# Closing waits of SyncE moved ahead of its fifth last output transfer

## The chip, the cores and the metric

The kernel runs on one core of a Trainium2 chip. The core has five engines with an instruction queue each: TensorE (PE), VectorE (DVE), ScalarE (ACT), GpSimd (POOL) and SyncE (SP). SyncE computes nothing: it issues transfers (DMAs) and waits. Engines and transfers are ordered by semaphores: an instruction raises one when it is done, a transfer raises its own by 16 when it has landed, and an engine that needs the result holds its queue until the semaphore has the value. The metric is the device time of one execution in microseconds. Before the change it was 160.47 us, the median of three runs (159.72, 160.47 and 160.56).

## The reference

The input x has 2048 rows of 448 values in bfloat16. It is normalized (`xn`), and two branches work on xn. Branch A is a linear recurrence with 448 complex states; branch B normalizes again and is a two-layer perceptron with 1792 hidden values. The result joins them with x:

```python
def _A_ref(x, Lambda_re, Lambda_im, B_re, B_im, C_re, C_im, log_dt, Dskip):
    Lam = Lambda_re + 1j * Lambda_im
    Lam_bar = jnp.exp(jnp.exp(log_dt) * Lam)
    Bu = jnp.einsum("bld,pd->blp", x + 0j, ((Lam_bar - 1.0) / Lam)[:, None] * (B_re + 1j * B_im))
    for t in range(L):
        h = Lam_bar[None, :] * h + Bu[:, t, :]        # collected in hseq
    return 2.0 * jnp.einsum("blp,dp->bld", hseq, C_re + 1j * C_im).real + x * Dskip
def _B_ref(x, w1, b1, w2, b2):
    h = gelu(jnp.einsum("bsd,df->bsf", layernorm(x), w1) + b1)
    return jnp.einsum("bsf,fd->bsd", h, w2) + b2
xn = layernorm(x)
out = x + _A_ref(xn, ...) * silu(_B_ref(xn, ...))
```

## The kernel before, in words

The 2048 rows are worked in four groups of 512, each in two blocks of 256 rows, and each block in its even and its odd rows. For a group the kernel normalizes the rows, transposes them by DMA (line 83), runs the perceptron's two layers on TensorE (lines 735 and 754), projects into the states (line 663), scans over time on VectorE, and multiplies the states back (`ym`, lines 787 to 793). `ym` ends with a product with the gate (line 796), a sum (line 799) and an output transfer (lines 808 and 813). A block's even and odd rows leave in one transfer of 224 KB, except in the last block, which leaves in three: 112 KB and 64 KB by SyncE's queue, 48 KB by ScalarE's.

No scheduler decides the order when the program is built. Every piece of work is recorded as a `Task` with the engine that does it and the buffers that it reads and writes; `link` turns these into dependences. `emit` walks a fixed list of task numbers, `ORDER`, and writes each task's instructions into its engine's queue. Ahead of a task it writes a wait for each semaphore that the task needs and that its engine hasn't yet waited for (lines 120 to 123); `seen` remembers, for each engine, how far it has waited. Each transfer has a semaphore of its own, named d0, d1 and so on (lines 76 to 85), so SyncE never learns of most transfers: the engines that read the data wait for them.

After the last task, lines 135 to 137 have SyncE wait for every semaphore at its final value that it hasn't already waited for. This is the closing list: 58 waits, which the build packs two to an instruction, so 29 instructions. Behind it stands the end of the block (line 288): a drain on SyncE and a barrier of all engines, released by GpSimd.

SyncE's queue ends with seven output transfers. The first two of these carry group 1. The other five are the two blocks of group 2 and the first block of group 3 (224 KB each), and the 112 KB and 64 KB of the last block. Each waits for the addition that makes its data. The last output transfer of the kernel, 48 KB, stands in ScalarE's queue.

Of the kernel before, what the change touches and what calls it, by code (L numbers as in the profile page):

```python
# [14 lines left out]
ENGS = ("pe", "act", "dve", "pool", "sp")  # L15
# [20 lines left out]
class Plan:  # L36
# [69 lines left out]
    def emit(self):  # L106
        self.link()
        for k in SECOND:
            self.tasks[k].choose(1)
        order = [self.tasks[k] for k in ORDER]  # L110
        assert len(order) == len(set(order)) == len(self.tasks)
        done = {}
        for t in order:
            eng, seen = self.engs[t.eng], self.seen[t.eng]
            need = {}
            for d in t.deps:
                sem, val = done[d]
                if need.get(sem, 0) < val:
                    need[sem] = val
            for sem, val in need.items():  # L120
                if seen.get(sem, 0) < val:
                    eng.wait_ge(self.sems[sem], val)
                    seen[sem] = val
            for k, fn in enumerate(t.ins):
                last = fn(eng)
                if t.chain and k < len(t.ins) - 1:
                    self.counts[t.eng] += 1
                    last.then_inc(self.sems[t.eng], 1)
                    eng.wait_ge(self.sems[t.eng], self.counts[t.eng])
                    seen[t.eng] = self.counts[t.eng]  # L130
            inc = 16 if t.sem not in ENGS else 1
            self.counts[t.sem] += inc
            last.then_inc(self.sems[t.sem], inc)
            done[t] = (t.sem, self.counts[t.sem])
        for sem, val in self.counts.items():
            if val and self.seen["sp"].get(sem, 0) < val:
                self.nc.sync.wait_ge(self.sems[sem], val)
# [781 lines left out]
```

## Time and profile before

| what | value |
|---|---|
| time, median of three runs | 160.47 us (159.72 to 160.56) |
| span of the profiled execution, first to last instruction | 158.54 us |
| last record of the same execution, from its first instruction | 160.47 us |
| TensorE busy | 148.2 us (93%) |
| VectorE busy | 136.2 us (86%) |
| end of the last VectorE addition | 155.81 us |
| issue of SyncE's last five output transfers | 140.62, 148.22, 153.76, 155.10, 155.62 us |
| issue of ScalarE's output transfer, and its landing | 155.85, 157.43 us |
| closing waits (line 137) | 29 instructions, 156.01 to 158.28 us |
| SyncE's drain at the block's end | 158.31 us |

Times are counted from the first instruction. "Issue" is when the queue starts the transfer's instruction; the landing is the last of its semaphore's 16 raises. A wait instruction is recorded from the moment its semaphores are met and the queue takes it, and takes 0.028 us itself. The page doesn't count waits and issues as busy time. The time of a whole execution is longer than its span, since work of the runtime lies around it: the semaphores are reset behind the last instruction, and the last such record is the one in the table.

### The profile page before, as it was taken

The page shows a single profiled execution, that of the slowest core. Times are in us where ns is not written, and L with a number is a line of the kernel's source. Part 1 is how long each engine was busy: PE and PEld are TensorE (multiplying, and loading weights), DVE is VectorE, ACT ScalarE, POOL GpSimd, SP SyncE. Part 2 cuts the span into 40 slices and gives each one's busy share as a digit, 9 for nine tenths or more (in the row PEclk, how much of TensorE's full clock was granted, in tenths as well). Part 3 has the DMA queues.
Part 4 walks back from the last instruction along what each step waited for, and adds up shares of the span by engine and source line. Part 5 has one row for each costly group of instructions (what it writes and reads, how often), then busy time and mean ns, then how long its engine had stood idle before and what let it go on. Part 6 is the DMA issues. An engine that isn't in the chain of part 4 may idle for free.

```text
span 158.5 us, 3106 instructions
## 1 busy us (share of the span) xinstructions
PE 148.2 (93%) x1130; PEld 87.9 (55%) x1130; DVE 136.2 (86%) x295; ACT 96.7 (61%) x180; POOL 38.8 (24%) x94
## 2 busy tenths in 40 slices
PE   0989999699999999999999999999999999999990
PEld 0977765244456656665554555675545665555560
DVE  1789997489898999989899799748999969999692
ACT  3589888998699667688989070233395774224110
POOL 5528622031902000054000018530000450002311
PEclk9999999999999999999999999999999999999998
DMA  4999966999998530000000517202740000010103
GB/s 110 269 300 290 316 187 130 202 233 246 110 170 166 60 76 0 2 0 0 4 0 0 102 27 160 80 0 45 51 142 0 0 4 0 0 58 4 58 2 118
DMA packets 31238, 14.75 MB, mean 93 GB/s; under 512 B 24752, under 2 KB 30774, under 8 KB 31222
## 3 DMA queue, kind: packets, MB, share of 16 engines
q1 hardware_dynamic: 30912, 14.26, 41.0%
q0 software_dynamic: 160, 0.23, 0.7%
q8 instruction: 9, 0.15, 0.4%
q10 hardware_dynamic: 150, 0.05, 0.1%
q14 instruction: 7, 0.06, 0.1%
HBM read 6.89 MB, written 1.84 MB: 55 GB/s over the span
## 4 chain that ended last, share of the span: by engine, by line
PE 67%; DMA 13%; SPq 9%; DVE 5%; issue 2%; ACT 2%; DVEq 0%
PE psum L754 20%; PE psum L735 15%; PE psum L663 14%; PE psum L787 10%; SPq L84 7%; DMA Bn<-in_A_B_im_dram 7%; PE psum L652 3%; PE psum L790 3%; DMA x_all<-in_A_x_dram 3%; DMA xnT<-xn_sb 3%; SPq L83 2%; ACT gT L739 1%; DVE t L796 1%; DVE tmp L799 1%; DVE o L757 1%
## 5 line engine op out<-in xcount | busy, mean ns | idle before, releaser
L735 PE MATMUL psum<-xn2T,w_sb 64*128 64x512 bf16 (+1 forms) x462 | 45.4, 345 | 2.3 <-DMA xn2T<-xn_sb 1.5
L754 PE MATMUL psum<-w_sb,gT 128*128 128x448 bf16 x224 | 44.5, 353 | 0.2 <-issue 0.2
L739 ACT ACTIVATE gT<-psum,b1f 128x512 bf16<-128x512 f32 (+1 forms) x66 | 36.1, 621 | 5.7 <-PE psum L735 5.3
L735 PEld LDWEIGHTS psum<-xn2T,w_sb 64*128 64x128 bf16 x462 | 25.1, 109 | 20.6 <-issue 2.5
L754 PEld LDWEIGHTS psum<-w_sb,gT 128*128 128x128 bf16 x224 | 21.6, 98 | 20.6 <-issue 0.8
L663 PE MATMUL psum<-xnT,BT 128*128 128x256 bf16 x196 | 24.1, 273 | 0.3 <-ACT gT L739 0.3
L663 PEld LDWEIGHTS psum<-xnT,BT 128*128 128x128 bf16 x196 | 18.6, 98 | 6.4 <-issue 1.6
L384 ACT ACTIVATE u_sb<-psum 128x512 bf16<-128x512 f32 (+2 forms) x21 | 9.9, 470 | 14.0 <-PE psum L663 13.9
L758 ACT ACTIVATE th<-o 128x448 f32<-128x448 f32 x16 | 9.1, 576 | 9.7 <-DVE o L757 9.6
L384 ACT ACTIVATE vs<-s_w 64x256 bf16<-64x256 f32 (+2 forms) x14 | 7.9, 565 | 11.4 <-DVE s_w L689 7.5
L771 POOL TENSOR_TENSOR xr<-xd,g_sb 128x448 f32<-128x448 bf16 x4 | 4.8, 1194 | 41.2 <-DVE tmp L799 23.2
L687 DVE TENSOR_TENSOR_SCAN s_w<-dk,vs 128x774 f32<-128x774 f32 x8 | 13.9, 1760 | 0.0
L796 DVE TENSOR_TENSOR t<-psum,g_sb 128x448 bf16<-128x448 f32 (+2 forms) x17 | 10.0, 590 | 4.3 <-PE psum L790 2.2
L459 ACT ACTIVATE xn_sb<-x_all,lnw 128x448 bf16<-128x448 bf16 (+2 forms) x18 | 11.4, 672 | 3.5 <-POOL xd L771 2.1
L787 PE MATMUL psum<-CZ,h_sb 128*128 128x448 bf16 x56 | 11.9, 353 | 0.0
L698 POOL TENSOR_TENSOR ang<-s_w,ang 128x16 f32<-128x16 f32 x3 | 2.0, 675 | 40.3 <-ACT s_w L696 20.7
L757 DVE TENSOR_TENSOR o<-psum,b2bc 128x448 f32<-128x448 f32 x16 | 9.8, 616 | 1.5 <-PE psum L754 1.5
L759 DVE SCALAR_TENSOR_TENSOR g_sb<-th,o 128x448 bf16<-128x448 f32 x16 | 10.4, 649 | 0.3 <-ACT th L758 0.2
L787 PE MATMUL psum<-CQ,h_sb 128*128 128x448 bf16 (+2 forms) x54 | 10.5, 332 | 0.0
L372 DVE BATCH_NORM_STATS2 lnst<-x_all 128x6 f32<-128x448 bf16 x12 | 7.4, 622 | 1.2 <-DMA x_all<-in_A_x_dram 1.2
L613 ACT ACTIVATE tmp<-Cr,cw 128x448 f32<-128x448 bf16 (+1 forms) x10 | 6.5, 664 | 2.6 <-DVE CZ L616 1.3
L787 PEld LDWEIGHTS psum<-CZ,h_sb 128*128 128x128 bf16 x56 | 5.4, 98 | 4.9 <-DVE o L757 0.4
(161 smaller groups left out, 194.1 us busy)
## 6 DMA issues: line engine op xcount, KB each, us to landing
out_dram<-tmp SPq DMA_DIRECT2D x7, 224.0 KB, 2.0
x_all<-in_A_x_dram SPq DMA_DIRECT2D x3, 448.0 KB, 5.1
w_sb<-in_B_w_dram SPq DMA_DIRECT2D x3, 448.0 KB, 8.7
w_sb<-in_B_w_dram SPq DMA_DIRECT2D x3, 384.0 KB, 5.4
vs<-in_A_C_re_dram SPq DMA_DIRECT2D x1, 392.0 KB, 7.6
vs<-in_A_C_im_dram SPq DMA_DIRECT2D x1, 336.0 KB, 10.8
Bn<-in_A_B_re_dram SPq DMA_DIRECT2D x1, 336.0 KB, 11.0
Bn<-in_A_B_im_dram SPq DMA_DIRECT2D x1, 336.0 KB, 11.3
```

The costliest lines, as they stand in the source:

```text
L84: return e.dma_start(out_ap, in_ap)
L384: kb.either(("act", [lambda e, o=o, i=i: e.activation(o, i, ACT.Copy) for o, i in pairs]), ("dve", [lambda e, o=o, i=i: e.tensor_copy(o, i ...
L459: ("act", [lambda e, o=o, i=i: e.activation(o, i, ACT.Identity, bias=nb, scale=rs) for o, i in parts], 0.75, 0.2)]
L663: fns = [lambda e, r=r, m=m, d=d: e.matmul(psum[:, 4, r * NK:(r + 1) * NK], BT[:, m, d, :], xnT[:, gx, d, :], start=(d == 0), stop=(d == 6 ...
L687: dve(lambda e, so=so, vi=vi: e.tensor_tensor_scan(so, dk[:].rearrange("p i c -> p (i c)"), vi, 0.0, ALU.mult, ALU.add), ["v", "vl", "dk", ...
L735: return lambda e: e.matmul(view(bk[k]), w1_sb[rows, d, fcol(2 * j + k)], rhs[rows, d, :, :], start=not second and n == 0, stop=second and ...
L739: act([lambda e, k=k: e.activation(gT[:, gb, 2 * j + k, :].rearrange("p (r c) -> p r c", r=2)[:, :, cols], view(bk[k]), ACT.Gelu_apprx_tan ...
L754: fns = [lambda e, fi=fi: e.matmul(psum[:, bk, 0:D], gT[:, gb, fi, q * 128:(q + 1) * 128], w2_sb[:, fi, :], start=(fi == 0), stop=(fi == N ...
L757: dve(lambda e: e.tensor_tensor(o2[:, fb, :], psum[:, bk, 0:D], b2bc[:], ALU.add), [f"ps{bk}", "b2bc"], [f"oo{fb}"], 0.62, prio - 76)
L759: dve(lambda e: e.scalar_tensor_tensor(out=g_sb[:, gs, :], in0=th[:, fb, :], scalar=1.0, in1=o2[:, fb, :], op0=ALU.add, op1=ALU.mult), [f" ...
L787: fns = [lambda e, k=k: e.matmul(psum[:, bk, c0:c1], h_sb[:, hb, k, k0:k0 + 128], cm[:, k, c0:c1], start=(k == 0), stop=False) for k in ra ...
L796: dve(lambda e: e.tensor_tensor(t3[:, fb, c0:c1], psum[:, bk, c0:c1], g_sb[:, gs, c0:c1], ALU.mult), [f"ps{bk}", f"g{gs}"], [f"t3{fb}_{c0} ...
```

## The change

`emit` picks the fifth last task of SyncE in the order (`settle`). When the walk comes to it, SyncE first waits for every transfer semaphore raised so far by the walk that it has not waited for, at its value then; semaphores of the engines (`ENGS`) are left out. `seen` records these waits, so the closing list at the end leaves them out. The order of the tasks on every engine is the same.

```diff
@@ -110,8 +110,14 @@
         order = [self.tasks[k] for k in ORDER]
         assert len(order) == len(set(order)) == len(self.tasks)
         done = {}
+        settle = [t for t in order if t.eng == "sp"][-5]
         for t in order:
             eng, seen = self.engs[t.eng], self.seen[t.eng]
+            if t is settle:
+                for sem, val in self.counts.items():
+                    if val and sem not in ENGS and seen.get(sem, 0) < val:
+                        eng.wait_ge(self.sems[sem], val)
+                        seen[sem] = val
             need = {}
             for d in t.deps:
                 sem, val = done[d]
```

## Prediction

> **What bounds the kernel now.** I read the page's first lines for the balance, then the chain of work that ended last, then SyncE's waits from 115 us on, and last the source lines of the closing waits (L137), of the block's end (L288) and of the output transfers.
>
> ```profile
> span 158.5 us, 3106 instructions
> PE 148.2 (93%) x1130; PEld 87.9 (55%) x1130; DVE 136.2 (86%) x295; ACT 96.7 (61%) x180; POOL 38.8 (24%) x94
> PE 67%; DMA 13%; SPq 9%; DVE 5%; issue 2%; ACT 2%; DVEq 0%
> ```
>
> TensorE is busy for 93% of the span and has most of the chain: it bounds the body, and the change touches none of its work. What matters is the tail. The end of the chain:
>
> ```profile
> 154.69 0.38 DVE tmp L799
> 155.07 0.28 DVE t L796
> 155.35 0.03 issue
> 155.38 0.02 DVEq L122
> 155.40 0.04 issue
> 155.44 0.37 DVE tmp L799
> ```
>
> The last engine work ends at 155.81, and 2.7 us remain in which no engine computes. They hold the last transfers, the closing waits and the block's end. By source line (start of first and last behind the durations):
>
> ```profile
> L137 SPq EVENT_SEMAPHORE  x29: 27/28/28, 156.0 to 158.2; - x29
> ...
> L288 SPq DRAIN  x1: 13/13/13, 158.3 to 158.3; - x1
> L288 SPq EVENT_SEMAPHORE  x1: 17/17/17, 158.5 to 158.5; - x1
> ```
>
> The output transfers from 155.7 us on, with the time to landing:
>
> ```profile
> L84 ACTq DMA_DIRECT2D out_dram<-tmp x1: 379/379/379, 155.8 to 155.8; - x1
> ...
> DMA to landing us min/median/max: 1.6/1.6/1.6
> ```
>
> ScalarE's transfer is issued at 155.85 and has landed at 157.43 by the trace's landing records; SyncE's last one (issued at 155.62) landed at 157.22. But the 29 closing waits run from 156.01, the last starts at 158.25, and the drain behind it at 158.31. So the last output has been in memory for 0.82 us when SyncE reaches its wait: 14 wait instructions start after 157.43, all on semaphores met long before. The tail is bound by SyncE walking its list.
>
> SyncE's waits from 115 us on:
>
> ```profile
> SPq L84 <- DVE tmp L799: 37.1, 3, 24.7
> SPq L84 <- DVE pa L681: 2.5, 1, 2.5
> SPq L84 <- DVE t L796: 1.3, 1, 1.3
> SPq L84 <- POOL tmp L799: 0.2, 1, 0.2
> ```
>
> The longest, 24.7 us, ends with the transfer at 140.62, the fifth last of SyncE: the place to which the waits go.
>
> **The change part by part.** The profile gives a span of 158.54 us; the last record of that execution stands 160.47 us after its first instruction, like the median of the three runs (159.72, 160.47, 160.56). I set the sum against 160.47, with 1.93 us around the span unchanged.
>
> *Taken from the end.* 58 waits stand two to an instruction. SyncE's order in the two programs shows what stays behind its last transfer: five instructions (nine waits: the last six output transfers and the final counts of TensorE, VectorE and ScalarE). 24 of 29 go. In the profile the steady ones start 0.062 us apart; the first seven stand 0.064 to 0.095 apart, and between the seventh (156.45) and the eighth (156.95) lies a pause of 0.43 us above that pace. Counted as instructions alone, 24 x 0.062 = 1.49 us, with the pause 1.9 us. But the landing now ends last, so not all of that is won.
>
> *What is late next.* The five remaining waits begin at 156.01 as before. By the landing records their transfers land at 155.72 and before, 156.76, 157.22 and 157.43, so four of the five are over before the last landing. The last then follows 0.02 us behind it: no row shows SyncE held here, but its wait at 22.79 us began 0.017 us after the landing at 22.776, and VectorE's and ScalarE's follow such landings by 0.02 to 0.03. Bounds: 0.017 us, and 0.095 if a full wait step comes on top; I take 0.02, from the rows of the same event. From there as now: 0.028 for the wait, 0.037 to the drain, 0.225 from the drain's start to the span's end. The new end is 157.425 + 0.02 + 0.028 + 0.037 + 0.225 = 157.735: 0.80 us less than 158.539 (0.73 at the upper bound).
>
> *Added ahead of the fifth last transfer.* 49 waits, 48 of them in 25 instructions (one more instruction on SyncE in all) and one riding on the transfer; the last of the 25 also holds the transfer's wait for VectorE. SyncE ends the issue before at 115.95 and is idle until 140.62. The youngest transfers waited for are the two outputs issued at 115.14 and 115.52, landed at 117.11 and 117.73. Even at 0.095 us each plus the pause, 25 take 2.8 us; if all came after the second landing, they would end at 120.6, 20 us ahead of the data. Cost zero; without that cover up to 2.8 us on this transfer, and even then nobody asks early: VectorE's wait for it stands at 150.12, 7.6 us after its landing at 142.55. Nothing else is queued on SyncE between the waits and the transfer.
>
> *The fifth last transfer itself.* Its VectorE wait moves to the instruction ahead of it, so its issue comes 0.046 to 0.075 us later (wait to next issue at 89.00 and at 22.79). The same 7.6 us cover it: zero. ScalarE's and GpSimd's queues are not moved past, and their transfers are those of before. The four later output transfers keep place and waits. On other instructions that wait for two semaphores the pair swaps its order; both must be met either way: zero.
>
> **Sum:** 160.47 - 0.80 = 159.67 us.
>
> A rule against the change: the Trainium skill ("DMA: Bandwidth & Descriptors", the table of fixed and variable time) gives a transfer about 2.0 us of fixed cost plus its bytes over 436 GB/s. For ScalarE's 48 KB that is an estimate of 2.11 us; the last landing would then be at 157.96, the gain 0.27, the time 160.20. The trace disagrees: this transfer took 1.58 us.
>
> **The rivals.**
>
> *Less pause (A).* The pause of 0.43 us is one event in one execution; it stands in the microsecond in which the DMA engines are busiest (0.70 from 156 to 157 us), and I can't tell it from an accident. Without it the closing waits of before end 0.43 earlier, and the change wins 0.80 - 0.43 = 0.37: 160.10. For it: the other 27 steps are even. Against it: the runs spread over 0.84 us, so executions may as well have longer pauses than this one, and then the change wins more.
>
> *Late landing (B).* The end now hangs on the landing, which was hidden behind 0.82 us of waits. The nine transfers of the output on SyncE took up to 2.2 us. If the last one takes that, it lands at 158.05, the gain is 0.18, the time 160.29. Against it: 2.2 is a row of 224 KB, and the three smallest took 1.6 to 1.7. The Trainium skill's rule above points this way.
>
> *Stalled issue, slower (C).* The five last transfers stand 25 instructions later in SyncE's stream. If the pause belongs to a place of the stream or to fetching it (fetches of 8 KB took 0.3 to 0.66 us here), it can fall right ahead of one of the last issues. One such stall of 0.43 to 0.66 us moves the last landing and eats most of the gain (160.1 to 160.33); the kernel gets slower from 0.80 us on, and two stalls of 0.66 in a row would give 160.47 + 1.32 - 0.80 = 160.99. Against it: SyncE has 20 idle us ahead of the first of them, and the pause lay before the eighth closing wait, which now stands in that idle stretch.
>
> *No effect (D).* If 2.7 us at the end went to something behind the block's end, the waits would not count: 160.47. Against it: the drain starts 0.037 us after the last wait.
>
> **How the numbers follow.** 0.5% is 0.80 us here, about what a measurement of this kernel can tell from no change, and the sum stands on that line. What tips it is the median of before: two of three runs stand 0.75 us and more above the lowest, and a closing list with longer or more pauses is one place where they can be; the landing as the new end drops all of them. Forecast (gain of 0.75 or more, up to 1.3 with a second pause, so 159.2 to 159.7): 0.62, of which 0.56 over the line. A 0.20, B 0.09, C 0.06 (0.04 slower, 0.02 same), D 0.03. A is over the line where the before it is compared with has a longer list: 0.04 of its 0.20. Faster 0.60, same 0.36, slower 0.04. The range runs from 159.1 (the forecast with a second pause, and 0.1 for the landing) to 160.3 (B).
>
> **What would show it.** In the changed profile: about five closing waits of the last loop behind the last output transfer, the last of them within 0.1 us of ScalarE's landing; 24 wait instructions between 116 and 121 us and one, which holds VectorE's wait too, at 140.6; the fifth last output transfer right behind it; the drain 1.6 to 1.7 us after ScalarE's issue, and 2.7 us of tail become 1.9. The prediction is wrong if an output issue after 150 us moves, if a landing takes over 2 us, or if the time around the span grows.

## The result

The changed kernel takes 159.25 us (median of 19 runs, 157.87 to 160.51), the kernel before 160.04 in the same comparison: ratio 0.9935, interval 0.991 to 0.9961. A second comparison gave 0.9942 (0.9912 to 0.9972). That is 1.04 and 0.93 us less, with about 0.4 to 0.5 us of uncertainty each way. Each ratio leaves out the runs that lie over 1.5% above the fastest of their kernel, here three of the changed kernel (160.29, 160.40 and 160.51, at a granted clock of 0.998 to 1.000) and one more in the second comparison, and none of the kernel before; over all runs the means lie 0.80 and 0.84 us apart. The change makes the kernel faster by about half a per cent.

The span of the profiled execution is no shorter (158.66 us against 158.54), because this execution is one of the longer ones: from 46 us on its body runs 0.94 us later than that of the kernel before, of which more in the last section. So I read the tail alone, from ScalarE's output issue to the end of the span, and beside it a second profile of the same kernel.

The closing waits of the changed kernel by source line: those ahead of the fifth last transfer (L119), those left at the end (L143), the drain and SyncE's last instruction (L294). First profile:

```profile
L119 SPq EVENT_SEMAPHORE  x24: 17/28/28, 116.9 to 118.9; - x24
...
L143 SPq EVENT_SEMAPHORE  x5: 17/28/28, 156.9 to 158.4; - x5
...
L294 SPq DRAIN  x1: 13/13/13, 158.4 to 158.4; - x1
L294 SPq EVENT_SEMAPHORE  x1: 17/17/17, 158.6 to 158.6; - x1
```

Second profile of the same kernel:

```profile
L119 SPq EVENT_SEMAPHORE  x24: 17/28/28, 115.3 to 117.3; - x24
...
L143 SPq EVENT_SEMAPHORE  x5: 17/28/28, 155.3 to 156.7; - x5
```

24 instructions have left the end and stand between 115 and 119 us, with 22 us of SyncE's idle time behind them. ScalarE's output transfer in the first profile and in the second, with its landing:

```profile
L84 ACTq DMA_DIRECT2D out_dram<-tmp x1: 378/378/378, 156.8 to 156.8; - x1
...
DMA to landing us min/median/max: 1.6/1.6/1.6
```

```profile
L84 ACTq DMA_DIRECT2D out_dram<-tmp x1: 378/378/378, 155.2 to 155.2; - x1
...
DMA to landing us min/median/max: 1.6/1.6/1.6
```

By the trace's records of start and landing, in us:

| | before | changed | changed, second |
|---|---|---|---|
| ScalarE's output issue | 155.846 | 156.783 | 155.151 |
| its landing | 157.425 | 158.355 | 156.722 |
| start of the last closing wait | 158.249 | 158.372 | 156.739 |
| end of the span | 158.539 | 158.662 | 157.030 |
| tail: issue to end of the span | 2.693 | 1.879 | 1.879 |

The last wait stood 0.82 us behind the last landing; now it follows 0.017 us behind it. What SyncE waits for from 115 us on, in the first profile of the changed kernel:

```profile
SPq L128 <- DVE tmp L805: 22.6, 1, 22.6
SPq L84 <- DVE tmp L805: 12.3, 2, 7.2
...
SPq L143 <- DMA out_dram<-tmp: 1.2, 3, 0.7
```

The idle time ahead of the fifth last transfer is 22.6 us now, 2 us of it went to the waits. The line of L143 is new: at the end SyncE waits for transfers, three times, which it never did before.

### The profile page after: what moved, and what is told of

Read it like the earlier page. It is cut to its first block, busy times and chain, and to the rows that moved or that the text cites. A ratio compares the mean times of both kernels' runs of the same rounds, so it can differ in the third digit from the quotient of the medians.

```text
span 158.7 us, 3107 instructions
## 1 busy us (share of the span) xinstructions
PE 148.0 (93%) x1130; PEld 88.2 (56%) x1130; DVE 136.2 (86%) x295; ACT 96.6 (61%) x180; POOL 38.9 (25%) x94
## 4 chain that ended last, share of the span: by engine, by line
PE 70%; DMA 14%; SPq 9%; DVE 2%; issue 2%; ACT 1%; DVEq 0%
PE psum L760 20%; PE psum L741 15%; PE psum L669 14%; PE psum L793 12%; DMA Bn<-in_A_B_im_dram 7%; SPq L84 7%; PE psum L796 4%; DMA x_all<-in_A_x_dram 4%; PE psum L658 3%; DMA xnT<-xn_sb 3%; SPq L83 2%; PE psum L799 1%; DVE lnst L378 1%; ACT gT L745 1%; ACT xn_sb L465 0%
```

## The experiments

"Tail" is the time from ScalarE's output issue to the end of the span. From one profile to another ScalarE's issue moved by up to 2.3 us, while the tail came out the same to 0.001 us in the two profiles of the changed kernel, and likewise in the two experiments with 16 and 80 redundant instructions. So I take one profile as enough for the tail; one pair below, with eight redundant instructions, differs by 0.23 us. "80th" counts the recorded instructions of SyncE from the start.

**No old waits.** The block of the change without its wait:

```diff
             if t is settle:
                 for sem, val in self.counts.items():
                     if val and sem not in ENGS and seen.get(sem, 0) < val:
-                        eng.wait_ge(self.sems[sem], val)
                         seen[sem] = val
```

> SyncE doesn't wait for the 49 old transfers at all, neither early nor late; five wait instructions stay at the end. Theory 1 (the gain is the walk through the closing list, and the moved waits are free): the tail from ScalarE's output issue to the end of the span is 1.88 us as in the changed kernel (before: 2.69), and the time is 0.5% to 0.7% under before, the same as the changed kernel's. Rival (the early waits themselves do something to the body or to the fifth last transfer): the time differs from the changed kernel's by more than the interval, or the issue of the later outputs moves against VectorE's additions.

The closing list that is left, by source line:

```profile
L142 SPq EVENT_SEMAPHORE  x5: 17/28/28, 155.5 to 156.9; - x5
```

Measured: tail 1.887 us, ratio 0.9961 (0.9928 to 0.9994). Same tail as with the waits moved, and a ratio whose interval holds those of the changed kernel. The 24 early wait instructions cost nothing that can be seen. The gain of 0.39% is below the expected 0.5% to 0.7%. Part of that lies behind the span: time less span is 1.80 us here and 1.73 for the kernel before (means of 12 and 23 runs), a loss of 0.07 to 0.08 us that the tail doesn't show and whose cause was not looked for. In the changed kernel it is not lost (1.72 against 1.73, 12 and 17 runs).

**Ahead of the last transfer.**

```diff
-        settle = [t for t in order if t.eng == "sp"][-5]
+        settle = [t for t in order if t.eng == "sp"][-1]
```

> The closing waits stand ahead of SyncE's last output transfer instead of the fifth last. 27 wait instructions then lie between the issues of the 112 KB and the 64 KB transfers, where SyncE is idle for only 0.2 us. Theory 1: the cover is gone: 27 x 0.062 + the pause 0.43 = 2.1 us of waits, the 64 KB issue comes 1.9 to 2.0 us later against ScalarE's (1.7 us behind it instead of 0.22 ahead), and the tail from ScalarE's issue to the end is 1.75 + 1.59 + 0.31 = 3.65 us (before 2.69, changed 1.88), the time about 0.6% over before. Rival (waits that are met cost SyncE nothing that counts, and the gain has another cause): the tail stays at 1.9 to 2.7 us.

By source line, the waits moved and the block's end:

```profile
L119 SPq EVENT_SEMAPHORE  x26: 17/28/28, 154.9 to 156.9; - x26
...
L294 SPq DRAIN  x1: 13/13/13, 158.8 to 158.8; - x1
```

The output transfers of the same kernel from 154 us on:

```profile
L84 SPq DMA_DIRECT2D out_dram<-tmp x2: 332/332/332, 154.5 to 157.1; - x2
L84 ACTq DMA_DIRECT2D out_dram<-tmp x1: 377/377/377, 155.3 to 155.3; - x1
```

The waits fill the time between the two issues, the 64 KB leave 1.82 us behind ScalarE's 48 KB, and the tail is 3.767 us (expected 3.65). Ratio 1.0046 (1.0011 to 1.008): slower. So it is the idle time ahead of the transfer that makes the moved waits free, and not the move.

**Where the pause belongs.** In the kernel before, redundant waits on the first two loads ahead of the fifth last transfer, 32 (16 instructions) or 160 (80); the closing list stays as before. The edit with 32:

```diff
+        settle = [t for t in order if t.eng == "sp"][-5]
         for t in order:
             eng, seen = self.engs[t.eng], self.seen[t.eng]
+            if t is settle:
+                for n in range(32):
+                    eng.wait_ge(self.sems[("d0", "d1")[n % 2]], 16)
```

> The kernel before, with 16 redundant wait instructions (on the first two loads, met since 4 us) ahead of the fifth last output transfer; the closing list stays at the end, complete. Theory P (the pause of 0.43 us belongs to a place in SyncE's stream, ahead of its 80th recorded instruction, where it stood in both profiles): the pause falls among the redundant waits, the 29 closing waits are evenly 0.062 us apart, and the tail from ScalarE's issue to the end shrinks from 2.69 to 2.26 us. Rival (the pause comes with the time or the transfers at the end): it stays in the closing list and the tail stays at 2.69 us.

> As the one with 16, with 80 redundant wait instructions. Theory P with a period: SyncE's 16th recorded instruction, the load at 7.79 us, also took 1 us more than its like, 64 instructions ahead of the 80th; then the next pause lies ahead of the 144th, among the 80 redundant waits (67 to 146), there are two pauses of about 0.43 us in them, and the closing list has none: tail 2.26 us. Rival (one single place): one pause only. All 80 take 80 x 0.062 + 0.43 to 0.86 = 5.4 to 5.8 us of the 24.7 idle ones, so the outputs don't move.

In the kernel before, the closing waits up to the pause and those behind it as far as 157.43 us:

```profile
L137 SPq EVENT_SEMAPHORE  x7: 28/28/28, 156.0 to 156.5; - x7
...
L137 SPq EVENT_SEMAPHORE  x8: 28/28/28, 156.9 to 157.4; - x8
```

With 16: the redundant waits up to the pause and behind it (L118; the 16th instruction also holds the transfer's own wait and is listed elsewhere), and the closing list (L141):

```profile
L118 SPq EVENT_SEMAPHORE  x12: 28/28/28, 116.4 to 117.1; - x12
...
L118 SPq EVENT_SEMAPHORE  x3: 27/28/28, 117.6 to 117.8; - x3
...
L141 SPq EVENT_SEMAPHORE  x29: 28/28/28, 156.3 to 158.0; - x29
```

With 80:

```profile
L118 SPq EVENT_SEMAPHORE  x79: 27/28/28, 115.3 to 120.6; - x79
...
L141 SPq EVENT_SEMAPHORE  x29: 28/28/28, 155.2 to 156.9; - x29
```

The 29 closing waits now take 1.7 us from the first start to the last, where before they took 2.2. The pause of 0.47 us stands ahead of the 80th instruction in both, at 117.61 and 116.56 us, 38 us ahead of the last transfers. The tail is 2.149 us in both; I had expected 2.26, because I had left out that the slower steps around the pause, of 0.064 to 0.095, go with it. The period of 64 instructions that I had guessed is not there: with 80 more, no second pause comes up to the queue's end, 103 instructions on; a longer period isn't ruled out. So 0.54 us of the change's 0.81 are the pause and its slow neighbours, and 0.27 are plain waits.

**Half of the waits.** As the change, but for the first 30 old waits only; 14 instructions stay at the end.

```diff
             if t is settle:
+                n = 30
                 for sem, val in self.counts.items():
-                    if val and sem not in ENGS and seen.get(sem, 0) < val:
+                    if val and sem not in ENGS and seen.get(sem, 0) < val and n:
                         eng.wait_ge(self.sems[sem], val)
                         seen[sem] = val
+                        n -= 1
```

> Of the 49 old waits 30 stand ahead of the fifth last output transfer and 19 stay in the closing list, which then has 14 wait instructions instead of 29 (before) or 5 (changed); the pause falls ahead. Theory L (the end is the later of the list's walk and the last landing): 14 x 0.062 = 0.87 us of walking ends before the last landing, so the tail from ScalarE's issue to the end is 1.88 us, the full gain of the changed kernel. Rival (each wait instruction at the end costs its 0.062 us): 9 more than in the changed kernel, so 1.88 + 0.56 = 2.44 us.

The closing list and the drain by source line:

```profile
L145 SPq EVENT_SEMAPHORE  x14: 27/28/28, 156.1 to 157.6; - x14
...
L296 SPq DRAIN  x1: 13/13/13, 157.6 to 157.6; - x1
```

ScalarE's output issue in it:

```profile
L84 ACTq DMA_DIRECT2D out_dram<-tmp x1: 377/377/377, 156.0 to 156.0; - x1
```

The 14 closing waits (L145) begin at 156.1 and the drain follows at 157.6, 1.7 us behind ScalarE's issue as in the changed kernel. Tail 1.887 us: nine more wait instructions at the end than in the changed kernel, and the same end. The end is the later of the two, the walk or the landing; beyond the landing, further waits taken away win nothing.

**Twice the waits.** In the closing list of the kernel before:

```diff
                 self.nc.sync.wait_ge(self.sems[sem], val)
+                self.nc.sync.wait_ge(self.sems["d0"], 16)
```

> The kernel before, with one redundant wait (on a load met since 4 us) for every closing wait: 58 wait instructions at the end instead of 29, nothing else changed. Theory 1 (SyncE walks the list at 0.062 us an instruction, and the walk sets the end): the tail from ScalarE's issue is 2.69 + 29 x 0.062 = 4.49 us and the time 1.8 us (1.1%) over before. Rival (waits that are met are only dear in the profile, or the landing sets the end): the time without a profile stays within 0.3% of before.

The old and the added closing waits by source line, whose instructions alternate:

```profile
L137 SPq EVENT_SEMAPHORE  x29: 27/28/28, 155.0 to 158.9; - x29
L138 SPq EVENT_SEMAPHORE  x29: 27/28/28, 155.1 to 159.0; - x29
```

Tail 4.444 us (expected 4.49). 29 more instructions cost 1.75 us, 0.060 each. The device times agree, but loosely: there are four runs, ratio 1.0163 (1.007 to 1.0257), so 1.1 to 4.1 us.

**The pause ahead of the last output.** The old waits dropped, and eight or nine redundant wait instructions ahead of the fifth last transfer, so that the 80th instruction is SyncE's last or its second last output issue.

```diff
             if t is settle:
                 for sem, val in self.counts.items():
                     if val and sem not in ENGS and seen.get(sem, 0) < val:
-                        eng.wait_ge(self.sems[sem], val)
                         seen[sem] = val
+                for n in range(16):     # 18 for nine
+                    eng.wait_ge(self.sems[("d0", "d1")[n % 2]], 16)
```

> No old waits, and eight redundant wait instructions ahead of the fifth last output transfer, so that SyncE's last output issue (64 KB) is the 80th recorded instruction, where the pause of 0.47 us stood in all six profiles. This is rival C of the prediction built on purpose. If the pause starts when the queue gets there: the issue before ends at 0.33 us behind its start, the 64 KB issue comes 0.47 us after that instead of 0.20, so 0.27 later, its landing 0.05 to 0.10 us after ScalarE's, and the tail from ScalarE's issue is 1.93 to 2.0 us (changed 1.88). If the queue fetches ahead while it waits: no delay, 1.88 us. In neither case does the kernel come near the tail of before, 2.69.

(Of those six profiles five show the pause; without old waits the queue ends ahead of its place.)

> The kernel with the pause ahead of SyncE's last output issue once more: its tail was 2.51 us, where I had expected 1.93 to 2.0. If that belongs to the arrangement (issue 0.28 us later, so that the 64 KB and the 48 KB move at the same time, and an instruction fetch of 8 KB 0.63 us behind the pause in the midst of them), the tail is 2.4 to 2.6 us again; if it was an accident, 1.9 to 2.0 us.

> One redundant wait instruction more than in the kernel with eight: the 80th recorded instruction of SyncE is now its second last output issue (112 KB), ahead of which it is idle for 1.0 us. If the pause starts when the queue gets there, it fits into this idle time, the issue is not delayed, the fetch behind it is over before the last two transfers move, and the tail from ScalarE's issue is 1.88 us. If the pause starts only when the instruction's semaphore is met, the 112 KB issue comes 0.47 us late, the 64 KB issue follows 0.3 to 0.35 us late, and the tail is 2.0 to 2.6 us.

With eight, first and second profile, the output transfers from 154 us on:

```profile
L84 SPq DMA_DIRECT2D out_dram<-tmp x3: 332/332/333, 155.1 to 157.2; - x3
L84 ACTq DMA_DIRECT2D out_dram<-tmp x1: 396/396/396, 157.2 to 157.2; - x1
...
DMA to landing us min/median/max: 1.7/2.0/2.2
```

```profile
L84 SPq DMA_DIRECT2D out_dram<-tmp x2: 332/332/332, 154.7 to 155.5; - x2
L84 ACTq DMA_DIRECT2D out_dram<-tmp x1: 396/396/396, 155.4 to 155.4; - x1
...
DMA to landing us min/median/max: 1.7/2.2/2.4
```

With nine:

```profile
L84 ACTq DMA_DIRECT2D out_dram<-tmp x1: 378/378/378, 155.4 to 155.4; - x1
...
DMA to landing us min/median/max: 1.6/1.6/1.7
```

With eight the last issue comes 0.466 us behind the end of the one before it instead of 0.195, as expected, 0.05 us behind ScalarE's instead of 0.22 ahead. But the landings are late by far more: ScalarE's 48 KB take 2.21 and 2.44 us instead of 1.57, and the tail is 2.512 and 2.743 us, once a little under the tail of before (2.693) and once over it. I had costed the later issue alone. By the packet records of the first profile the two transfers now run through each other (the 64 KB from 0.88 to 1.47 us behind ScalarE's issue, the 48 KB from 0.97 to 1.61; in the changed kernel 0.61 to 0.97 and 0.89 to 1.20), and an instruction fetch of 8 KB falls into the same time (0.69 to 1.26, and 1.03 to 1.34 in the second). Of ScalarE's extra 0.63 and 0.87 us, 0.40 and 0.60 lie ahead of its last data packet's end and 0.23 and 0.27 between that and the landing. How much is the fetch and how much the two transfers was not separated. With nine the pause fits into the idle 1.0 us ahead of the 112 KB transfer, and the tail is 1.869 us.

**The changed kernel again.**

> The changed kernel once more, unaltered, with another profile and more rounds. Theory 1 (the whole gain is the tail's 0.81 us, and the other part of the 1.04 us of the first comparison is the spread of the body, which waits at 30 us for a transposing DMA): the tail from ScalarE's issue is 1.88 us again and the ratio comes out nearer to 0.995 than to 0.990. Rival (a further gain of 0.2 us or more, in the body or around the span): the ratio stays at 0.9935 or lower, and the body up to ScalarE's issue is shorter than in the other profiles.

Measured: tail 1.879 us, ratio 0.9942 (0.9912 to 0.9972). The ratio lies between the two expectations and its interval holds both. The means over all runs lie 0.84 us apart, close to the tail's 0.81, and the profiles show no other gain: the time from 46 us to ScalarE's issue and the time around the span are those of before.

## Why the prediction was right or wrong

- *What bounds the tail: right.* The walk through the list set the end and not the landing. Moved waits, dropped waits and half of them moved give 1.88 to 1.89 us, twice the waits 4.44.
- *The size of the step: right.* 0.80 us were forecast from 0.02 for the wake, 0.028, 0.037 and 0.225; the tail shrank by 0.814, and the wake took 0.017. "24 wait instructions between 116 and 121 us" stood at 116.9 to 118.9 and 115.3 to 117.3.
- *What it costs ahead of the fifth last transfer: right.* Nothing (no old waits: same tail), and without the cover 1.07 us of tail (ahead of the last transfer: slower than before).
- *Less pause (A): a wrong rival.* I gave 0.20 to a pause that is an accident of one execution. In ten of the twelve profiles it stands ahead of the 80th recorded instruction of SyncE. In the other two it can't be seen: with nine redundant instructions it fits into the idle time there, and without old waits or redundant ones the queue ends before that place. Both profiles with an unchanged queue up to there, the kernel before and the one with twice the waits, have it among the closing waits. So there is no ground for a list of before without it. My two readings for A were loose as well: the other steps are not even (0.059 to 0.095 us, the slow ones around the pause), and 0.70 is the busiest microsecond of the tail alone. Without the pause and its slow neighbours 0.27 us would be left to win, not 0.37.
- *The step that failed: the base of the sum, 160.47, and "what tips it is the median of before".* The sum set the gain against the median of three runs. These stood high: 19 runs give 160.04. 160.04 less 0.81 is 159.23, and 159.25 was measured, so the 0.42 us between the forecast 159.67 and the result are that base, and not the gain. I took the height and the spread of the three runs for longer or more pauses in the list, and built the lean to "faster" on it. The list's steps agree to 0.01 us in the two profiles that have it whole up to the pause and behind it, and the spread comes about before 46 us (last section). That profile and median both gave 160.47 was chance: the 1.93 us reach to the last record of the resets, while the runs' times are only 1.73 us above their spans (17 runs of the kernel before, 1.68 to 1.78). On that scale the profiled execution was one of 160.27.
- *The single figure.* 0.80 of 160.47 is 0.499%, a hair under the bound that I had named for a change that can be told. The text leaned to faster (0.60), the figure by itself says no change. The measured 0.65% is past the bound. The tail's own 0.81 us (0.51% of 160.04) lies inside both intervals, and the means over all runs give 0.50% and 0.52%. So the 0.1 to 0.2 us by which the two ratios go further are not shown to be a gain, and "faster" came true for another reason than the one that I gave: a gain of the size of the sum, which the runs could just tell.
- *Late landing (B): wrong.* The 48 KB landed in 1.57 us in both profiles of the changed kernel, as before. The fixed 2.0 us of the Trainium skill ("DMA: Bandwidth & Descriptors", the table of fixed and variable time, in the section on transfers that GpSimd issues) would, by my estimate, have left a gain of 0.27; the trace disagrees again, for a transfer that ScalarE issues.
- *Stalled issue (C): real, and not here.* The pause does belong to a place of the stream, as C supposed. With it ahead of the last issue the tail is 0.63 to 0.86 us longer, most of the gain or all of it. The change put 25 instructions ahead of the last issues, and that place now lies in the idle stretch. Eight put it ahead of the last output.

## What to carry to other kernels

Look at what the engine that closes the kernel does between the last landing and the drain: a list of waits that are all met still costs its steps (0.06 us each here), and was free where the queue was idle. Move only until the landing ends last; beyond that, moving the further waits brought nothing. And where instructions are moved in a queue, its slow places move relative to the work: look for a gap that stands at the same instruction in every profile, and for what now stands there.

## What the runs showed of the hardware that I had not expected

**A fixed slow place in SyncE's queue.** Ahead of its 80th recorded instruction SyncE stood still for 0.465 to 0.468 us, whether that instruction came at 117 us or at 157, among waits or ahead of an issue. An instruction fetch of 8 KB follows, in nine of the ten profiles that show the pause 0.62 to 0.65 us behind its end, in one 0.98. That fits the border between two fetched blocks of the stream, but no run varied the size of a block. The Trainium skill ("Runtime: NRT & Kernel Launch", Instruction fetch mechanics) says that the sequencer fetches ahead by itself and that crossing a block is mostly hidden; if the place is such a border, these traces disagree by 0.47 us, on a queue whose instructions follow each other every 0.06.

**Two small output transfers at the same time.** With their data moving through each other, and a fetch in between, 48 KB took 2.2 to 2.4 us to land, against 1.57 when they ran one behind the other.

**The spread of the profiles comes about before 46 us.** From TensorE's 381st matmul, at 43.4 to 45.6 us, to ScalarE's last issue the twelve profiles take 111.37 to 111.57 us. The largest part of the spread ahead of it is TensorE's wait at about 30 us for a transposed tile, here in the first and in the second profile of the changed kernel:

```profile
31.45 1.92 PE L741 MATMUL psum<-xn2T,w_sb 64*128 64x512 bf16 x16 [2.37 <-DMA xn2T<-xn_sb]
```

```profile
30.73 2.57 PE L741 MATMUL psum<-xn2T,w_sb 64*128 64x512 bf16 x22 [1.30 <-DMA xn2T<-xn_sb]
```

It lasted 0.6 to 2.4 us over the profiles, and ScalarE's last issue came between 154.8 and 157.2 us, mostly in step with it. It isn't the whole: of the 0.94 us by which the first profile of the changed kernel runs later than that of the kernel before, 0.42 are there behind this wait, and 0.52 come from short waits of TensorE at 43.9 and 45.2 us. What delays the transpose (its data, its place behind the loads) was not tried.
